# Linear attention and a gated feed-forward layer on one core: two batches' tail rows together, batch 0's k through two DMA queues, and a new order of the first batch

## The chip, the core and the metric

The kernel runs on 1 core of one Trainium2 chip. The metric is the device time of one execution in microseconds (us). TensorE (PE) multiplies matrices, VectorE (DVE) and ScalarE (ACT) work on elements, GpSimd (POOL) issues nearly all loads here, and SyncE (SP) issues the stores and the transposing DMAs. The engines run at the same time, each through its own list of instructions in order, and wait for each other through semaphores.

## The reference

Shapes: 8 batches, 8 heads, 576 rows, head size 64; the feed-forward layer takes 4608 rows of 512, widens them to 2048 and goes back to 512. Inputs and output are float32.

```python
phi = lambda x: np.where(x > 0, x, np.exp(x) - 1.0) + 1.0
q_p, k_p = phi(q), phi(k)
kv  = np.einsum('bhsd,bhse->bhde', k_p, v);  z = np.sum(k_p, axis=2)
num = np.einsum('bhsd,bhde->bhse', q_p, kv)
den = np.einsum('bhsd,bhd->bhs', q_p, z)[..., None] + 1e-06
x = (num / den).transpose(0, 2, 1, 3).reshape(4608, 512)
h = x @ w_in
g = h * (1.0 / (1.0 + np.exp(-beta * h)))
out = g @ w_out
```

## The kernel before

**Tiles.** The 576 rows of a batch are 4 tiles of 128 rows (t = 0..3) and a tail of 64 rows (t = 4). The main rows go through the feed-forward layer batch by batch. The 8 tails are collected in `xT_tail` (512 columns) and go through it at the end as a ninth "batch" (b = 8).

**Stages.** The order is written out by hand (`tc.manual_schedule()`). For each b there is a stage h(b): 16 groups of 128 hidden columns, 4 matmuls each into a PSUM bank, then Silu on ACT into `g_sb` (`h_mm` L453, `silu` L445). Then stage y(b): 64 matmuls with `w_out` (`y_mm` L505), four results of 128x512, copied and stored. A dictionary (`plan`) says after which group a piece of the next batch's attention is put: `relu`, `exp_`, `phi`, `v_copy` (v with a column of ones, `vaug`), `kv_mm` (L344, sums of k and v, with `kv_evac` into `kv_bd`), then for each tile t `num_mm` (L399: four matmuls), `num_norm` (three DVE instructions, L413 to L415, giving `xs`), and the transposition of `xs`: by PE in batches 0 to 2 (`x_trans` L433 and a copy L370 or L372), by a DMA of SP from batch 3 on (L419). The tail of each batch does the same with 64 rows, and ends in 64 columns of `xT_tail`.

**Loads.** All loads but that of beta are issued by POOL, and they cast float32 to bfloat16 on the way; the order is that of the text: k, q and v of batch 0 (in pieces, `load_nine` L129), four `w_in`, `w_out` in eight pieces of float32 (some lie for a while in buffers of later batches: `xqk[2]`, `xT[1]`, `xT[2]`, `g_sb[1]`), k and q of batch 1, v of batch 1, then batch 2 and so on. A load waits until the one eight places before it has landed. `w_out_scale` (L212) turns float32 `w_out` into bfloat16 on DVE.

**The start.** Batch 0 is split into 9 rows per partition (j = 0..8) with 4 heads in each half of the partitions, so that every load is wide. k comes as one piece of 9 rows for each half, q as j 0..3 and j 4..8, v as j 0..5 and j 6..8. ACT makes `exp` (L256), DVE `relu` (L264) and the minimum (L270); PE adds up k (L307 with `ones`), transposes q (L282), adds up k and v (L307 with `v9`); ACT and DVE empty the banks. Meanwhile PE runs matmuls on zeros (`warm`, L575). `beta` is loaded by SP, transposed by PE at the start and worked up by five small DVE instructions (`make_beta`, L199 to L205). On DVE the `relu` of q's second part (L264) comes ahead of the first `num_norm`.

Of the kernel before, what the change touches and what calls it, by code (L numbers as in the profile page):

```python
# [16 lines left out]
def kernel(  # L17
# [99 lines left out]
    def nine(a, spec):  # L117

        names = " ".join(spec)
        flat = a.rearrange("p a b c -> p (a b c)")  # L120
        size = {"h": HH, "j": N9, "d": D}
        n = size["h"] * size["j"] * size["d"]
        return flat[:, 0:n].rearrange(f"p ({names}) -> p {names}", **size)

    q9 = nine(xqk[0][:, 0], "hjd")
    k9 = nine(xqk[0][:, 1], "hjd")
    v9 = nine(vraw[0], "hjd")

    def load_nine(dst, src, h0=0, h1=HH, j0=0, j1=N9):  # L129
        for g in range(2):  # L130
            nc.gpsimd.dma_start(  # L131
                out=dst[g * TAIL : (g + 1) * TAIL, h0:h1, j0:j1, :].rearrange(
                    "p h j d -> p h (j d)"
                ),
                in_=src[0, g * HH + h0 : g * HH + h1, :, :]
                .rearrange("h (p j) d -> p h j d", j=N9)[:, :, j0:j1, :]
                .rearrange("p h j d -> p h (j d)"),
            )
# [3 lines left out]
    nc.scalar.activation(small[:, 0:1], small[:, 0:1], ACTF.Exp)  # L142
    nc.vector.memset(g_sb[0][:, FC - 1, :], 0.0)  # L143
    clear_tail(1)
    nc.vector.memset(vraw[1][TAIL:P, :, NJ, :], 0.0)
    beta_row = consts.tile([FC, P], F32)
    nc.sync.dma_start(out=beta_row, in_=moe_beta.rearrange("(c p) -> c p", p=P))

    identity = consts.tile([P, P], BF16)
    ident16 = consts.tile([FC, FC], F32)  # L150
    load_nine(k9, k)
    load_nine(q9, q, j1=4)
    make_identity(nc, identity)
    make_identity(nc, ident16)
    load_nine(v9, v, j1=6)
    load_nine(v9, v, j0=6)
    load_nine(q9, q, j0=4)
    for i in range(4):
# [88 lines left out]

    x0 = {0: q9, 1: k9}

    def work9(tag, **kw):  # L250
        return nine(work.tile([P, H, NT, D], BF16, tag=tag, name=tag, **kw), "jhd")

    def exp0(a, j0, j1):
        if j0 == 0:
            st["e0", a] = work9("e", bufs=3)
        nc.scalar.activation(  # L256
            st["e0", a][:, j0:j1].rearrange("p j h d -> p h j d"), x0[a][:, :, j0:j1],
            ACTF.Exp,
        )

    def relu0(a, j0, j1):
        if j0 == 0:
            st["r0", a] = work9("r")
        nc.vector.tensor_scalar(  # L264
            st["r0", a][:, j0:j1].rearrange("p j h d -> p h j d"), x0[a][:, :, j0:j1],
            0.0, 1.0, ALU.max, ALU.add,
        )

    def phi0(a, j0, j1):
        nc.vector.tensor_tensor(  # L270
            st["p0"][a][:, j0:j1], st["r0", a][:, j0:j1], st["e0", a][:, j0:j1], ALU.min
        )

    def q_trans0(t, banks, c0):


        for jj in range(2 if t < NJ else 1):
            for a in range(2):
                for g in range(2):
                    gs = slice(g * TAIL, (g + 1) * TAIL)  # L280
                    m0 = c0 + a * P + jj * TAIL
                    nc.tensor.matmul(  # L282
                        banks[:, g, m0 : m0 + TAIL],
                        st["p0"][0][gs, 2 * t + jj, 2 * a : 2 * a + 2, :],
                        identity[gs, gs],
                        is_transpose=True, start=True, stop=True, skip_group_check=True,
                    )

    def q_out0(t, banks, c0, dve):
        n = rows(t)  # L290
        src = banks[:, :, c0 : c0 + 2 * P].rearrange("p g (a n) -> p g a n", a=2)
        dst = st[0, "qT"][:, t].rearrange("p (g a) n -> p g a n", g=2)
        copy(dst[:, :, :, :n], src[:, :, :, :n], dve)

# [4 lines left out]
    def kv_mm0(kvp, j0, j1, of_v):  # L299


        for j in range(j0, j1):
            for a in range(2):
                for g in range(2):
                    gs = slice(g * TAIL, (g + 1) * TAIL)
                    cols = kv_cols(kvp, g, a)
                    nc.tensor.matmul(  # L307
                        cols[:, :, 0:D] if of_v else cols[:, :, D],
                        st["p0"][1][gs, j, 2 * a : 2 * a + 2, :],
                        v9[gs, 2 * a : 2 * a + 2, j, :] if of_v else ones[gs],  # L310
                        start=(j == 0 and a == 0 and not of_v),
                        stop=(j == N9 - 1 and a == 1 and of_v),
                        skip_group_check=True,
                    )

    def kv_evac0(kvp):
        for g in range(2):
# [75 lines left out]
    def num_mm(b, t):  # L393
        n = rows(t)
        nps = att_banks()
        st[b, "n", t] = nps
        for p in range(KC):
            c0 = (p % 2) * 2 * (D + 1)
            nc.tensor.matmul(  # L399
                nps[:n, p // 2, c0 : c0 + 2 * (D + 1)],  # L400
                st[b, "qT"][:, t, p, :n],
                kv_bd[b % 2][p // 2][:, p % 2],
                start=True, stop=True, skip_group_check=True,
            )

    def num_norm(b, t):
        n = rows(t)
        den = work.tile([P, 2, 4], F32, tag="den", name="den")
# [8 lines left out]
        )  # L417
        if by_dma(b):
            nc.sync.dma_start_transpose(  # L419
# [3 lines left out]
    def x_dst(b, t):  # L423
        if t < NJ:
            return xT[b % 3][:, t]
        return xT_tail[:, :, b * TAIL : (b + 1) * TAIL]

    def x_trans(b, t, wide=False, dve=False):
        n = rows(t)
        xv = st[b, "xs", t].rearrange("p a h d -> p (a h d)")  # L430
# [49 lines left out]

    out0 = out[0:S, :].rearrange("(p j) m -> p j m", j=N9)

    def tail_rows(b):
        if b == 0:
            return out0[:, N9 - 1, :]
        return out[b * S + MAIN : (b + 1) * S, :]

    def store(b, t, y_sb):
        if b < B:
            if b == 0:  # L490
                for i in range(2):
                    nc.sync.dma_start(
                        out=out0[:, 2 * t + i, :], in_=y_sb[i * TAIL : (i + 1) * TAIL, :]
                    )
# [88 lines left out]
    def F(f, *a, **k):  # L583
        return lambda: f(*a, **k)

    begin(0)
    st["warm"] = mm_bank([P, 512])
    warm(10)
    beta_trans()
    make_beta()  # L590
    warm(20)
    st["p0"] = [
        nine(st[0, "p"][:, a].rearrange("p j (h d) -> p j h d", h=H), "jhd")
        for a in range(2)
    ]
    exp0(1, 0, 5)
    exp0(1, 5, N9)
    exp0(0, 0, 4)
    relu0(1, 0, 5)
    relu0(1, 5, N9)  # L600
    phi0(1, 0, 5)
    relu0(0, 0, 4)
    phi0(1, 5, N9)
    phi0(0, 0, 4)
    kvp = [mm_bank([P, 512]) for _ in range(2)]
    kv_mm0(kvp, 0, N9, False)
    qb = att_banks(BF16)
    q_trans0(0, qb, 0)
    q_trans0(1, qb, 256)
    q_out0(0, qb, 0, False)  # L610
    q_out0(1, qb, 256, False)
    kv_mm0(kvp, 0, 6, True)
    kv_mm0(kvp, 6, N9, True)
    kv_evac0(kvp)
    st["warm"] = mm_bank([P, 512])
    warm(1)
    num_mm(0, 0)
    num_mm(0, 1)
    exp0(0, 4, N9)
    relu0(0, 4, N9)  # L620
    silu_table()
    num_norm(0, 0)
    phi0(0, 4, 6)
    warm(4)
    x_trans(0, 0, dve=True)
    qb2 = att_banks(BF16)
    q_trans0(2, qb2, 0)
    q_out0(2, qb2, 0, False)
    num_norm(0, 1)
    phi0(0, 6, N9)  # L630

# [4 lines left out]

    def tidy0():
        clear_tail(0)
        nc.vector.memset(vraw[0][TAIL:P, :, NJ, :], 0.0)

    def q_rest0():
        q_trans0(3, qb2, 256)
        q_trans0(4, qb2, 512)
        q_out0(3, qb2, 256, False)
        q_out0(4, qb2, 512, False)

# [5 lines left out]
        {  # L652
            3: [F(x_trans, 0, 1), F(num_mm, 0, 2), F(num_norm, 0, 2), F(q_rest0)],
            5: [F(num_mm, 0, 3), F(num_norm, 0, 3)],
            7: [F(x_trans, 0, 2)],
            8: [F(num_mm, 0, 4), F(num_norm, 0, 4)],
            9: [F(x_trans, 0, 3), F(tidy0)],
            12: [F(x_trans, 0, 4)],
            17: [F(w_out_scale, 0), F(w_out_scale, 1)],
# [33 lines left out]
            1: [F(x_trans, 1, 3)],  # L693
            3: [F(x_trans, 1, 4)],
            8: [F(begin, 2), F(relu, 2, 0)],
# [12 lines left out]
        11: [F(num_mm, 2, 0), F(num_norm, 2, 0)],  # L708
        12: [F(num_mm, 2, 1), F(num_norm, 2, 1), F(x_trans, 2, 0, wide=True)],
        13: [F(num_mm, 2, 2), F(num_norm, 2, 2), F(x_trans, 2, 1, wide=True)],  # L710
        14: [F(num_mm, 2, 3), F(num_norm, 2, 3)],
    })

    for b in range(2, B + 1):
# [3 lines left out]
        if b == 2:  # L718
# [3 lines left out]
            plan = {  # L722
                0: [F(x_trans, 2, 2), F(num_mm, 2, 4), F(num_norm, 2, 4)],
                1: [F(x_trans, 2, 3)],
                3: [F(x_trans, 2, 4)],
            }
# [14 lines left out]
        if n < B:  # L741
            for t in range(NT):
                plan[1 + 2 * t] = [F(num_mm, n, t)]
# [32 lines left out]
```

## Time and profile before

| what | value |
|---|---|
| median of 5 runs (lowest to highest) | 296.69 us (296.07 to 297.36) |
| profiled execution, its own time | 296.69 us |
| span of that execution in the profile | 294.9 us |
| busy time: PE / DVE / ACT / POOL | 283.6 / 124.0 / 175.0 / 52.4 us |
| moved by POOL's queue / by SP's queue | 20.45 / 16.20 MB |

The page of the profile gives busy times of the engines, the span in 40 slices of 7.37 us, and the chain of waits that ended last. A timeline lists the instructions in order of time: start, length, engine, line, what is written and read, and in brackets how long the engine had been idle and which engine or DMA ended that. Matmuls overlap each other in the records, so the length of one is not what it costs in a row of many; the chain shows what a row costs. The span leaves out 1.79 us of the execution's time.

### The profile page before, as it was taken

The numbers are of one execution on the slowest core, as the hardware profiler recorded it, in microseconds if no ns is written. First come the engines' busy times: TensorE is split into PE (matmuls) and PEld (weight loads), VectorE is DVE, ScalarE is ACT, GpSimd is POOL, SyncE is SP. The second block draws the span as 40 slices with busy tenths as digits, with TensorE's granted clock in tenths as the row PEclk, the third lists the DMA queues.
The fourth block names the chain that finished last, engine by engine and source line by source line (L and its number), as shares of the span: only waits on it lengthen the run. The fifth ranks groups of instructions, "written<-read, shape, count | busy, mean of one in ns | idle before, by whom it ended". The sixth has DMA issues, their size and how long they took to land.

```text
span 294.9 us, 4750 instructions
## 1 busy us (share of the span) xinstructions
PE 283.6 (96%) x1891; PEld 143.8 (49%) x1912; DVE 124.0 (42%) x261; ACT 175.0 (59%) x234; POOL 52.4 (18%) x72
## 2 busy tenths in 40 slices
PE   8779999999899999999999999999999999999994
PEld 3457445644465544445444544454445444444444
DVE  4675488504365174616461646164715400110012
ACT  2798786889988770778077808790770077018500
POOL 8824575540003200320033000000000000000000
PEclk9999999999999999999999999999999999999999
DMA  7999999999637993699369955024502400120032
GB/s 103 189 207 345 253 278 192 257 192 191 94 142 101 175 137 107 129 179 150 98 129 159 161 107 124 2 72 115 127 0 72 118 36 0 38 90 16 0 73 71
DMA packets 72310, 37.09 MB, mean 126 GB/s; under 512 B 40912, under 2 KB 66784, under 8 KB 72288
## 3 DMA queue, kind: packets, MB, share of 16 engines
q0 software_dynamic: 38912, 20.45, 47.8%
q1 hardware_dynamic: 33216, 16.20, 23.1%
q8 instruction: 15, 0.25, 0.3%
q10 hardware_dynamic: 160, 0.13, 0.2%
q14 instruction: 7, 0.06, 0.1%
HBM read 36.71 MB, written 9.44 MB: 156 GB/s over the span
## 4 chain that ended last, share of the span: by engine, by line
PE 76%; ACT 9%; DMA 7%; issue 3%; POOL 2%; DVE 2%; ACTq 0%; POOLq 0%
PE mm L453 36%; PE mm L505 33%; DMA vraw<-in_v_dram 5%; ACT e L229 3%; PE att L399 3%; DMA xqk<-in_q_dram 2%; PE att L344 1%; ACT g L445 1%; ACT L229 1%; PE mm L537 1%; PE att L453 1%; POOL xqk L131 1%; ACT L581 1%; POOL vraw L131 1%; DVE qk_p L242 0%
## 5 line engine op out<-in xcount | busy, mean ns | idle before, releaser
L445 ACT ACTIVATE g<-mm,beta_c 128x512 bf16<-128x512 f32 (+2 forms) x156 | 97.3, 633 | 87.9 <-PE mm L453 87.7
L505 PE MATMUL mm<-w_out,g 128*128 128x512 bf16 x541 | 126.7, 379 | 1.2 <-issue 0.3
L453 PE MATMUL mm<-xT,w_in 128*128 128x512 bf16 (+2 forms) x560 | 108.1, 349 | 0.6 <-DVE xT L370 0.3
L453 PEld LDWEIGHTS <-w_in 128*128 128x128 bf16 x656 | 61.9, 98 | 61.5 <-DMA w_in<-in_moe_w_in_dram 0.4
L505 PEld LDWEIGHTS <-g 128*128 128x128 bf16 x560 | 52.8, 97 | 58.3
L515 DVE COPY y_sb<-mm 128x512 f32<-128x512 f32 x27 | 18.7, 692 | 70.5 <-PE mm L505 69.1
L229 ACT ACTIVATE e<-xqk 128x2560 bf16<-128x2560 bf16 x14 | 31.9, 2329 | 0.1
L415 DVE TENSOR_TENSOR xs<-att,rden 128x512 bf16<-128x512 f32 (+1 forms) x40 | 27.6, 690 | 1.4
L242 DVE TENSOR_TENSOR qk_p<-r,e 128x2560 bf16<-128x2560 bf16 x14 | 20.9, 1490 | 13.1 <-ACT e L229 12.4
L72 POOL DMA_DIRECT2D vraw<-in_v_dram x7 | 7.0, 998 | 84.2 <-DVE vaug L370 78.4
L355 DVE CAST kv_bd<-att 64x130 bf16<-64x130 f32 x28 | 8.2, 292 | 32.2 <-PE att L344 31.8
L413 DVE TENSOR_SCALAR den<-att 128x8 f32<-128x8 f32 (+1 forms) x40 | 6.5, 162 | 31.4 <-PE att L399 31.2
L399 PE MATMUL att<-kv_bd,q_pT 128*128 128x130 bf16 (+1 forms) x160 | 15.8, 221 | 1.5 <-DVE kv_bd L370 0.7
L399 PEld LDWEIGHTS <-q_pT 128*128 128x128 bf16 (+1 forms) x160 | 11.6, 100 | 11.1 <-DVE xs L415 2.4
L453 PE MATMUL mm<-xT_tail,w_in 128*128 128x512 bf16 x63 | 13.9, 379 | 0.1
L237 DVE TENSOR_SCALAR r<-xqk 128x2560 bf16<-128x2560 bf16 x14 | 11.6, 836 | 3.7 <-DMA xqk<-in_q_dram 2.2
L575 PE MATMUL mm<-g 128*128 128x512 bf16 x34 | 9.4, 435 | 1.2 <-DVE g L143 1.2
L229 ACT ACT_TABLE_LOAD x7 | 9.0, 1283 | 0.1
L414 DVE RECIPROCAL rden<-den 128x8 f32<-128x8 f32 (+1 forms) x40 | 8.1, 201 | 1.4
L256 ACT ACTIVATE e<-xqk 128x1280 bf16<-128x1280 bf16 (+1 forms) x4 | 4.4, 1155 | 5.9 <-DMA xqk<-in_k_dram 5.3
L72 POOL DMA_DIRECT2D xqk<-in_k_dram x7 | 6.8, 977 | 5.5 <-DMA w_in<-in_moe_w_in_dram 2.0
L72 POOL DMA_DIRECT2D xqk<-in_q_dram x7 | 6.3, 900 | 6.3 <-ACT g L445 2.6
(71 smaller groups left out, 140.2 us busy)
## 6 DMA issues: line engine op xcount, KB each, us to landing
out_dram<-y_sb SPq DMA_DIRECT2D x28, 256.0 KB, 2.3
xqk<-in_k_dram POOLq DMA_DIRECT2D x7, 512.0 KB, 10.7
xqk<-in_q_dram POOLq DMA_DIRECT2D x7, 512.0 KB, 11.6
vraw<-in_v_dram POOLq DMA_DIRECT2D x7, 512.0 KB, 11.3
w_in<-in_moe_w_in_dram POOLq DMA_DIRECT2D x4, 512.0 KB, 10.8
g<-in_moe_w_out_dram POOLq DMA_DIRECT2D x4, 512.0 KB, 10.9
out_dram<-y_sb SPq DMA_DIRECT2D x14, 128.0 KB, 5.2
xqk<-in_moe_w_out_dram POOLq DMA_DIRECT2D x2, 512.0 KB, 14.4
```

Source lines behind the costliest of these rows:

```text
L72: eng.dma_start(out=dst[:, :, 0:NJ, :].rearrange("p h j d -> p h (j d)"), in_=src[b, :, 0:MAIN, :].rearrange("h (p j) d -> p h (j d)", j=NJ),)
L229: nc.scalar.activation(st[b, "e", a][:, h0:h1], xqk[b % NX][:, a, h0:h1], ACTF.Exp)
L237: nc.vector.tensor_scalar(st[b, "r", a][:, h0:h1], xqk[b % NX][:, a, h0:h1], 0.0, 1.0, ALU.max, ALU.add)
L242: nc.vector.tensor_tensor(st[b, "p"][:, a].rearrange("p j (h d) -> p h j d", h=H)[:, h0:h1], st[b, "r", a][:, h0:h1], st[b, "e", a][:, h0: ...
L355: nc.vector.tensor_copy(kv_bd[b % 2][i][gs, :, g, :], st[b, "kvp"][gs, 2 * i : 2 * i + 2, :])
L399: nc.tensor.matmul(nps[:n, p // 2, c0 : c0 + 2 * (D + 1)], st[b, "qT"][:, t, p, :n], kv_bd[b % 2][p // 2][:, p % 2], start=True, stop=True ...
L415: nc.vector.tensor_mul(xs[:n], nv[:, :, :, 0:D], rden[:n, :, :, None].to_broadcast([n, 2, 4, D]))
L445: nc.scalar.activation(g_sb[b % 2][:, ff, c0:c1], hp[:, c0:c1], ACTF.Silu, scale=beta_c[:, ff : ff + 1],)
L453: nc.tensor.matmul(hp[:, c0:c1], w_in_sb[ff // 4][:, kc, (ff % 4) * P : (ff % 4 + 1) * P], x[:, t0:t1, kc, :] if b < B else x[:, kc, c0:c1 ...
L505: nc.tensor.matmul(yp, g_sb[b % 2][:, ff, t * P : (t + 1) * P], w_out_sb[ff // 4][:, ff % 4, :], start=(ff == 0), stop=(ff == FC - 1),)
L515: nc.vector.tensor_copy(y_sb, yp)
L575: nc.tensor.matmul(st["warm"], g_sb[0][:, FC - 1, 0:P], g_sb[0][:, FC - 1, :], start=True, stop=True, skip_group_check=True,)
```

## The change

- **Joint tails.** The tails of batches 2i and 2i+1 are worked on together: `num_mm` of the tail is called for the odd batch alone, and issues eight matmuls, alternately for batch 2i (rows 0 to 63 of the bank) and 2i+1 (rows 64 to 127). One `num_norm` with 128 rows follows, and one transposing DMA of SP into 128 columns of `xT_tail`, for batches 0 to 2 too, whose tails PE transposed before.
- **k by two queues.** k of batch 0 is cut into j 0..4, loaded by POOL as before, and j 5..8, loaded by SP without a cast as float32 into a part of `g_sb[1]` (`k_last`). `beta` is loaded by ACT's queue instead of SP's. v is cut at 5 instead of 6.
- **Order in batch 0.** `make_beta` comes behind the minimum; 25 instead of 30 matmuls on zeros; the minimum of q's first part in two pieces; the sums over k's first part ahead of those over its second; q's tile 1 is transposed behind the sums. The first `num_norm` comes ahead of the `relu` of q's second part. In h(0) the pieces lie after other groups, and q's tiles 2 to 4 are transposed together, two of them copied by DVE.
- **Batch 2.** All four copies behind `x_trans` go to DVE; the second `x_trans` comes one place later.
- In POOL's list every load stands where it stood.

```diff
+    k_last = g_f[:, 0 : HH * (N9 - KF) * D].rearrange(
+        "p (h j d) -> p h j d", h=HH, j=N9 - KF
+    )
...
+    load_nine(k_last, k, KF, N9, eng=nc.sync)
...
-    nc.sync.dma_start(out=beta_row, in_=moe_beta.rearrange("(c p) -> c p", p=P))
+    nc.scalar.dma_start(out=beta_row, in_=moe_beta.rearrange("(c p) -> c p", p=P))
...
-    load_nine(k9, k)
-    load_nine(q9, q, j1=4)
+    load_nine(x9[1][:, :, 0:KF], k, 0, KF)
+    load_nine(x9[0][:, :, 0:QF], q, 0, QF)
...
     def num_mm(b, t):
-        n = rows(t)
         nps = att_banks()
         st[b, "n", t] = nps
         for p in range(KC):
             c0 = (p % 2) * 2 * (D + 1)
-            nc.tensor.matmul(
-                nps[:n, p // 2, c0 : c0 + 2 * (D + 1)],
-                st[b, "qT"][:, t, p, :n],
-                kv_bd[b % 2][p // 2][:, p % 2],
-                start=True, stop=True, skip_group_check=True,
-            )
+            for i in range(1 if t < NJ else 2):
+                bb, n, r0 = (b, P, 0) if t < NJ else (b - 1 + i, TAIL, i * TAIL)
+                nc.tensor.matmul(
+                    nps[r0 : r0 + n, p // 2, c0 : c0 + 2 * (D + 1)],
+                    st[bb, "qT"][:, t, p, :n],
+                    kv_bd[bb % 2][p // 2][:, p % 2],
+                    start=True, stop=True, skip_group_check=True,
+                )
...
-        if by_dma(b):
+        if by_dma(b) or t == NJ:
...
-        return xT_tail[:, :, b * TAIL : (b + 1) * TAIL]
+        return xT_tail[:, :, (b - 1) * TAIL : (b + 1) * TAIL]
...
+    num_norm(0, 0)
-    exp0(0, 4, N9)
-    relu0(0, 4, N9)
+    exp9(0, QF, N9)
+    relu9(0, QF, N9)
     silu_table()
-    num_norm(0, 0)
-    phi0(0, 4, 6)
     warm(4)
     x_trans(0, 0, dve=True)
+    num_norm(0, 1)
+    phi9(0, QF, 6)
+    phi9(0, 6, N9)
     qb2 = att_banks(BF16)
-    q_trans0(2, qb2, 0)
-    q_out0(2, qb2, 0, False)
-    num_norm(0, 1)
-    phi0(0, 6, N9)
...
-            3: [F(x_trans, 0, 1), F(num_mm, 0, 2), F(num_norm, 0, 2), F(q_rest0)],
-            5: [F(num_mm, 0, 3), F(num_norm, 0, 3)],
-            7: [F(x_trans, 0, 2)],
-            8: [F(num_mm, 0, 4), F(num_norm, 0, 4)],
-            9: [F(x_trans, 0, 3), F(tidy0)],
-            12: [F(x_trans, 0, 4)],
+            1: [F(x_trans, 0, 1)],
+            3: [F(q_rest)],
+            5: [F(num_mm, 0, 2), F(num_norm, 0, 2)],
+            7: [F(num_mm, 0, 3), F(num_norm, 0, 3)],
+            8: [F(x_trans, 0, 2)],
+            10: [F(x_trans, 0, 3, dve=True), F(tidy)],
...
             1: [F(x_trans, 1, 3)],
-            3: [F(x_trans, 1, 4)],
...
-        12: [F(num_mm, 2, 1), F(num_norm, 2, 1), F(x_trans, 2, 0, wide=True)],
-        13: [F(num_mm, 2, 2), F(num_norm, 2, 2), F(x_trans, 2, 1, wide=True)],
-        14: [F(num_mm, 2, 3), F(num_norm, 2, 3)],
+        12: [F(num_mm, 2, 1), F(num_norm, 2, 1), F(x_trans, 2, 0, wide=True, dve=True)],
+        13: [F(num_mm, 2, 2), F(num_norm, 2, 2)],
+        14: [
+            F(x_trans, 2, 1, wide=True, dve=True), F(num_mm, 2, 3), F(num_norm, 2, 3),
+        ],
...
-                0: [F(x_trans, 2, 2), F(num_mm, 2, 4), F(num_norm, 2, 4)],
-                1: [F(x_trans, 2, 3)],
-                3: [F(x_trans, 2, 4)],
+                0: [F(x_trans, 2, 2, dve=True)],
+                1: [F(x_trans, 2, 3, dve=True)],
...
-            for t in range(NT):
+            for t in range(NT if n % 2 else NJ):
```

## The prediction

> **What bounds the kernel now.** First the page: the slices, then the chain that ended last by engine.
>
> ```profile
> PE   8779999999899999999999999999999999999994
> PEclk9999999999999999999999999999999999999999
> DMA  7999999999637993699369955024502400120032
> ...
> PE 76%; ACT 9%; DMA 7%; issue 3%; POOL 2%; DVE 2%; ACTq 0%; POOLq 0%
> ```
>
> From about 85 us on PE is the bound (no idle slice but the last, granted clock 1.0 throughout): there only PE work that goes away counts. Before that the DMA engines are busy in every slice to 74 us (ten slices), so I look at that stretch by windows (busy us of each engine, granted clock, share of the 16 DMA engines, GB/s; over 1 because transfers overlap):
>
> ```profile
> 2.00:3.00 1.00, 1.00 (x4) 0.39 (x3) 0.89 (x4) 0.23 (x2) 1.00 (x3) 1.00 0.34 25
> 3.00:5.00 2.00, 2.00 (x7) 0.61 (x5) 0.71 (x7) 0.00 (x0) 1.85 (x7) 1.00 1.03 141
> 5.00:7.50 2.50, 2.50 (x13) 1.21 (x13) 0.95 (x5) 0.00 (x0) 2.50 (x5) 1.00 1.23 187
> 17.00:42.00 25.00, 24.52 (x188) 14.88 (x190) 15.10 (x30) 22.02 (x39) 11.87 (x15) 1.00 1.29 276
> 42.00:52.00 10.00, 9.18 (x110) 5.55 (x110) 8.67 (x22) 6.00 (x10) 6.68 (x8) 1.00 1.50 211
> 52.00:74.00 22.00, 21.95 (x152) 11.82 (x153) 6.74 (x9) 19.65 (x29) 6.71 (x7) 1.00 1.53 213
> ```
>
> One queue feeds them without a hole from 3 us on; before 3 us they are nearly empty. Then the timeline, at the places where PE waits for a load:
>
> ```profile
> 7.52 1.27 ACT L256 ACTIVATE e<-xqk 128x1280 bf16<-128x1280 bf16 x1 [5.28 <-DMA xqk<-in_k_dram]
> ...
> 16.92 0.90 PEld L453 LDWEIGHTS <-w_in 128*128 128x128 bf16 x16 [0.41 <-DMA w_in<-in_moe_w_in_dram]
> ...
> 42.18 0.83 DVE L370 COPY vaug<-vraw 128x2560 bf16<-128x2560 bf16 x1 [0.42 <-DMA vraw<-in_v_dram]
> ...
> 43.06 0.82 PE L344 MATMUL att<-vaug,qk_p 128*64 128x65 bf16 x40 [0.20 <-DVE vaug L370]
> ...
> 79.49 0.40 PE L399 MATMUL att<-kv_bd,q_pT 128*128 128x130 bf16 x4 [0.66 <-DMA q_pT<-qk_p]
> ```
>
> k is in at 7.5; h(0) starts at 16.9 when `w_in` and the first `xT` arrive together; in y(0) PE needs batch 1's v (landed 42.05) for `kv_mm` at 43.06; in y(1) it needs batch 2's transposed q at 79.49. So the kernel is three stretches: to 43 us loads, then PE with one wait for a transposing DMA, then PE alone. The sum is made against the profiled execution, 296.69 us for a span of 294.9; the median of the five runs is the same 296.69.
>
> **The change part by part.**
>
> *k by two queues.* Beta, alone on SP's queue, is issued at 0.75 and the trace's packet records show it moving at 2.05; k's first packets on POOL's queue move at 2.96. So a second queue can start 0.9 us earlier, in the empty window. Against it stands more packet work. The records give, per packet, 0.107 us for 1152 bytes (0.145 in the first half of k), 0.072 for 640 bytes, 0.060 for 512 bytes (which read 1024 bytes), 0.098 for 1024 bytes (which read 2048). k was 512 x 0.107 = 54.8 engine-us. It becomes 512 x 0.072 plus 512 float32 packets of 1024 bytes, which no load of before has: between 0.060 and 0.098, so 67.6 to 87.0. The sum rises by 12.8 to 32.2 engine-us, at about 20 per us (share 1.23 x 16) 0.6 to 1.6 us. The cut of v gives 0.1 back, and the slow first half of k (256 x 0.038 / 19 = 0.5 us) may fall into the empty window. Best: 0.9 + 0.5 + 0.1 - 0.6 = 0.9 us gained; worst: 0.9 + 0.1 - 1.6 = 0.6 lost. I take 0.6 gained: the 512-byte packet reads as many bytes, so it is the nearest row. As the DMA engines have no hole until 74 us and POOL's list is unchanged, every later load moves by this, batch 1's v too: **-0.6 us**.
> The Trainium skill (DMA: Bandwidth & Descriptors, "Issuing engines are not separate DMA queues") speaks against this: a second issuing engine saves only issue time, since all share 16 DMA engines. By the rule the term would be near nothing, which is the first rival; the row that bears on it is the empty window from 2 to 3 us.
>
> *First norm ahead, new order in h(0).* On DVE the `relu` of q's second part (0.61 us, waiting for its load to 14.18) goes from in front of `den` to behind `xs`; the xT copy would end near 15.5 instead of 16.87. Next late is `w_in` at 16.87 - 0.6: h(0) starts near 16.3. Inside h(0) the tail's four `num_mm` (0.35 in the chain) and its `x_trans` (0.22) go, eight transpositions of q's tile 2 come in (0.29). The waits for `xT` and `q_pT` (0.26, 0.16) may go or come. PE would reach y(0) a us or more early, but PE already waited at 43.06 for v of batch 1, and that comes 0.6 early only. So beyond the loads this is worth **0**; without the cover (v early) it would be 0.5 to 1. The same cover hides a late start of up to half a us.
> At nothing too: beta's issue on ACT (idle to 7.52; were beta later than PE's 5.08, only matmuls on zeros wait); `make_beta`, 1.08 us, on DVE while it idled 1.52 us before the `kv_bd` copy at 12.93; `relu` from float32, by the `w_out` scaling (0.44 for 512 columns) 0.9 instead of 0.56 for 1024, beside ACT's three `exp` of 3.2 us; five fewer zero matmuls. New waits: PE now stands before v's first part with k's second sums and q's transposition queued behind, done before v's second part lands at about 12. A later `kv_bd` delays `xT`, which has 0.8 us until `w_in`.
> PE idles somewhat more between 9 and 16 us; the trace shows clock 1.00 there with PE busy for 3.1 of 5 us (12 to 17). The Trainium skill (TensorE: Matmul & The Clock Gate, "Part 1: The HAM clock gate") says that about 3.4 us of idleness halves the clock. No gap that I work out is so long; by the rule nothing is lost.
>
> *Joint tails.* What four of them cost, from the chain, in order of time:
>
> ```profile
> 97.74 0.75 PE att L344 x40
> ...
> 110.74 0.35 PE att L399 x4
> ```
>
> A pair of tails cost 0.70. Eight alternating matmuls of 130 columns: at most 0.70 again; at least as L344, which alternates between the same halves: 0.75/(40 x 65) = 0.29 ns a column, so 0.30. I take 0.40, near L344, with the 0.12 that four tail matmuls cost over four full ones (0.23) added. In h(1): 0.35 and an `x_trans` of 0.22 become 0.40: **-0.2** (-0.27 to +0.13). Batches 3 to 7, all on PE's path: 5 x 0.35 = 1.75 becomes 3 x 0.40 = 1.20: **-0.55** (-0.85 to +0.35). The norms and DMAs saved lie beside PE work.
>
> *Batch 2.* h(2) loses its tail `num_mm` and `x_trans`; PE took 2.97 us from 85.08 to 88.05, of which 16 matmuls (1.74) and two `x_trans` (0.44) stay: up to 0.8 less. In y(1) ACT is busy with `exp` and table until 81.7, and PE waited 0.29 for ACT's xT copy at 82.91; with the copies on DVE the chain is three norms (1.13 each) and copies (0.42), and h(2) starts 0.1 earlier: together **-0.85** (-0.57 to -0.9).
>
> *The wait at 79.49.* q's transposing DMA was issued at 70.14 and landed 9.3 us later (5.6 in the median), beside POOL's loads, which run to 74.8. After: the issue comes 0.8 earlier, the loads' end only 0.1, because the new transposing DMA of tails 0 and 1 (512 packets of 0.023 us, 0.5 us of all engines) goes among them. 0.7 us more overlap; I count half: **+0.35** (-0.3, if the wait goes, to +0.7).
>
> "Loads of batch 2 not held back": each stands in POOL's list where it stood, and waited for loads ahead of it (1.9 us at 36.4), so nothing beyond the term above.
>
> Sum: -0.6 - 0.2 + 0.35 - 0.85 - 0.55 = -1.85; 296.69 - 1.85 = **294.8 us**.
>
> **The rivals.**
> 1. *The second queue wins nothing*, as the DMA engines are shared. For: the saturated windows. Against: the empty one. Without the 0.6 the sum is -1.25: 295.4; at its bad end 296.0.
> 2. *The eight matmuls don't overlap.* A pair costs 0.70: h(1) +0.13, later batches +0.35. Sum -0.6 + 0.13 + 0.35 - 0.85 + 0.35 = -0.6: 296.1. Against: L344.
> 3. *Slower: two queues get in each other's way.* If all packets of k take 0.145 us, as its first half did, k costs 148 engine-us instead of 65, 83/19 = 4.4 us more, less 0.9 of early start: batch 1's v lands 3.5 us late, and PE stands at `kv_mm`. +3.5 - 0.2 - 0.85 - 0.55 = +1.9: 298.6. It decides from v 1.6 us late (no gain); beyond 2.5 it is slower by 0.9 us. For: two rings at a time have not been seen in this stretch. Against: from 5 us on, three loads queued together move at full rate.
>
> **How the numbers follow.** This kernel's measurement tells 0.3% (0.9 us) from no change: below 295.8 is faster, above 297.6 slower. Forecast 0.62, rival 1 0.15, rival 2 0.10, rivals 1 and 2 together 0.03, rival 3 0.10. Faster: 0.59 of the forecast, 0.09 of rival 1, 0.03 of rival 2: 0.71. Slower: 0.10. Same: 0.19. All good ends together give -0.9 - 0.27 - 0.3 - 0.9 - 0.85 = -3.2: 293.5 at the low end; all bad ends +1.2: 297.9. I stop at 297.2, leaving out rival 3 and the last of the bad ends.
>
> **What would show it.** First `exp` before 7.0 instead of 7.52; `w_in` awaited no longer than 16.4; PE's `kv_mm` of batch 1 near 42.4, waiting for v; `num_mm` of batch 2 near 79.0; h(2) from 84.4, its second half from about 86.7; the entries for tails in the chain become one for two batches, of about 0.40; the period of two batches from 101 us shorter by 0.3. I am wrong if batch 1's v does not land earlier, or if PE's waits between 43 and 85 us grow.

## The result and the profile after

| | before | changed kernel |
|---|---|---|
| median of the runs (lowest to highest) | 296.39 us (296.05 to 297.36, 45 runs) | 297.92 us (295.87 to 299.0, 25 runs) |
| ratio to before, 95% interval | | 1.004 (1.0029 to 1.0051) |
| profiled execution / its span | 296.69 / 294.9 us | 298.14 / 296.4 us |

The change makes the kernel slower by 0.4%, 1.5 us; 294.8 was predicted, and the highest time of the range was 297.2. The first part of the page that answers to the one shown of before (busy tenths and granted clock in 40 slices of 7.41 us, then the chain by engine):

```profile
PE   8889999999599999999999999999999999999994
...
PEclk9899999999989999999999999999999999999999
DMA  8999999999924996599359955023502400020032
...
PE 88%; DMA 6%; DVE 2%; POOL 2%; issue 1%; POOLq 0%
```

PE has a slice of 5 where it had 9: the eleventh, 74 to 81.5 us. The slice behind it shows a lower clock, and so does the second. The DMA engines are full in the eleventh slice too (9, was 6). The windows (columns as before: busy us of PE, PEld, DVE, ACT, POOL, then clock, DMA share, GB/s) put sizes to it:

```profile
2.00:3.00 1.00, 1.00 (x4) 0.39 (x3) 0.89 (x4) 0.23 (x2) 1.00 (x2) 1.00 0.55 101
...
12.00:17.00 5.00, 4.17 (x39) 2.32 (x39) 2.94 (x11) 4.12 (x7) 2.77 (x4) 0.66 1.25 206
...
42.00:52.00 10.00, 9.64 (x114) 5.98 (x114) 8.56 (x22) 5.96 (x11) 6.09 (x8) 1.00 1.53 200
...
78.00:82.00 4.00, 0.42 (x5) 0.43 (x6) 0.00 (x0) 2.84 (x3) 0.00 (x0) 0.86 0.55 67
81.00:85.00 4.00, 3.42 (x19) 2.07 (x20) 1.62 (x6) 0.60 (x1) 0.00 (x0) 0.59 0.00 0
```

The second queue does fill the window from 2 to 3 us (DMA share 0.55, was 0.34). From 42 to 52 PE works more than before (9.64, was 9.18). From 78 to 82 PE stands, with half of the DMA engines busy, and from 81 to 85 it runs at a clock of 0.59. The same places in the timeline as before:

```profile
7.68 1.27 ACT L269 ACTIVATE e<-xqk 128x1280 bf16<-128x1280 bf16 x1 [5.45 <-DMA xqk<-in_k_dram]
...
17.14 0.62 PE L477 MATMUL mm<-xT,w_in 128*128 128x128 bf16 x8 [0.72 <-DMA w_in<-in_moe_w_in_dram]
...
41.37 0.83 DVE L391 COPY vaug<-vraw 128x2560 bf16<-128x2560 bf16 x1 [0.39 <-DMA vraw<-in_v_dram]
...
42.52 0.82 PE L365 MATMUL att<-vaug,qk_p 128*64 128x65 bf16 x40
...
53.96 1.39 SPq L443 DMA_TRANSPOSE xT_tail<-xs  x1
...
69.10 7.00 SPq L409 DMA_TRANSPOSE q_pT<-qk_p  x1
...
81.58 0.62 PE L423 MATMUL att<-kv_bd,q_pT 128*128 128x130 bf16 x4 [3.76 <-DMA q_pT<-qk_p]
```

To 69 us the changed kernel is ahead: batch 1's v lands 0.8 us earlier (41.37, was 42.18), and q's transposing DMA is issued 1.0 earlier (69.10, was 70.14). But PE waits for that DMA to 81.58, 3.76 us instead of 0.66: it takes 12.4 us to land, not 9.3. The chain of waits (start, length, what) shows what this is worth:

```profile
69.10 12.43 DMA q_pT<-qk_p
...
82.19 1.71 PE mm L529 x4
...
88.46 0.44 PE mm L477 x4
...
100.17 0.75 PE att L365 x40
...
113.17 0.35 PE att L423 x8
```

Four `y_mm` at 82.19 take 1.71 us; in a row at full clock four take 0.86. h(2) starts at 88.46, 3.2 later than before, where the chain has it at 85.25:

```profile
85.25 0.44 PE mm L453 x4
```

Then the gains come: `kv_mm` of batch 3 is 2.4 late (100.17 against 97.74), and the end 1.5 late. The eight tail matmuls cost 0.35, what four did. So all of the loss arises between 69 and 88 us, at q's DMA and right behind it.

### The profile page after: what moved, and what is told of

It reads as the page before. It is cut to its first block, busy times and chain, and to the rows that moved or that the text cites. A ratio compares the mean times of both kernels' runs of the same rounds, so it can differ in the third digit from the quotient of the medians.

```text
span 296.4 us, 4705 instructions
## 1 busy us (share of the span) xinstructions
PE 283.5 (96%) x1874; PEld 143.4 (48%) x1895; DVE 122.3 (41%) x257; ACT 171.5 (58%) x225; POOL 51.5 (17%) x72
## 4 chain that ended last, share of the span: by engine, by line
PE 88%; DMA 6%; DVE 2%; POOL 2%; issue 1%; POOLq 0%
PE mm L477 40%; PE mm L529 37%; DMA q_pT<-qk_p 4%; PE att L423 4%; PE att L477 2%; DMA vraw<-in_v_dram 2%; PE att L365 2%; PE mm L561 1%; DVE xs L439 1%; POOL xqk L135 1%; PE mm L457 1%; PE mm L599 1%; POOL vraw L135 1%; PE att L401 0%; DVE rden L438 0%
## 5 line engine op out<-in xcount | busy, mean ns | idle before, releaser
L245 DVE TENSOR_TENSOR qk_p<-r,e 128x2560 bf16<-128x2560 bf16 x14 | 20.9, 1491 | 12.4 <-ACT e L232 11.7
L439 DVE TENSOR_TENSOR xs<-att,rden 128x512 bf16<-128x512 f32 x36 | 24.9, 691 | 1.5 <-DVE rden L438 0.2
L437 DVE TENSOR_SCALAR den<-att 128x8 f32<-128x8 f32 x36 | 5.9, 163 | 32.7 <-PE att L423 32.5
L423 PE MATMUL att<-kv_bd,q_pT 128*128 128x130 bf16 (+1 forms) x160 | 15.2, 230 | 4.0 <-DMA q_pT<-qk_p 3.8
L537 ACT ACTIVATE y_sb<-mm 128x512 f32<-128x512 f32 x8 | 4.8, 597 | 7.6 <-PE mm L529 7.6
L438 DVE RECIPROCAL rden<-den 128x8 f32<-128x8 f32 x36 | 7.3, 203 | 1.2
```

The lines of the kernel that those rows point to most:

```text
L245: nc.vector.tensor_tensor(st[b, "p"][:, a].rearrange("p j (h d) -> p h j d", h=H)[:, h0:h1], st[b, "r", a][:, h0:h1], st[b, "e", a][:, h0: ...
L423: nc.tensor.matmul(nps[r0 : r0 + n, p // 2, c0 : c0 + 2 * (D + 1)], st[bb, "qT"][:, t, p, :n], kv_bd[bb % 2][p // 2][:, p % 2], start=True ...
L439: nc.vector.tensor_mul(xs[:n], nv[:, :, :, 0:D], rden[:n, :, :, None].to_broadcast([n, 2, 4, D]))
```

## The experiments

The kernel before ran beside each group at 296.35 to 296.63 us. Theory A was: the transposing DMA of tails 0 and 1 (L443, issued at 53.96), which runs among the loads, delays them so far that their end meets q's transposing DMA. The expectations name its rivals.

**1. Tails 0 and 1 transposed by PE again.**

```diff
-        if by_dma(b) or t == NJ:
+        if by_dma(b) or (t == NJ and b > 1):
...
             1: [F(x_trans, 1, 3)],
+            3: [F(x_trans, 1, 4)],
```

> The changed kernel, but the joint tail of batches 0 and 1 is transposed by PE in h(1) again (four matmuls, one copy of ACT), not by a DMA of SP. Theory A (that DMA, issued at 54 us among the saturated loads, makes the loads end about 3 us later; they then overlap q's transposing DMA of batch 2, PE stands 3.8 us at its num_mm and the clock halves): PE's wait there under 1.2 us, loads' end near 75 us, clock 1.0 after 80 us, time 294.0 to 294.9. Theory B (not the tail's DMA but the earlier start of everything, by k's second queue, makes stores, loads and q's transposing DMA meet): the wait stays near 3.8 us, time 297 to 298. Theory C (the half clock from 12.9 to 16.3 us in the first batch costs the time): 297 to 298.

Measured: 294.32 us (294.21 to 294.45), ratio 0.9924 (0.991 to 0.9939). This one DMA costs 3.6 us (297.92 - 294.32). In this profile q's DMA is awaited for no time at all (in those of experiments 2, 6 and 8, which have no DMA of tails among the loads either, for 0.78 to 0.94 us):

```profile
78.86 0.41 PE L423 MATMUL att<-kv_bd,q_pT 128*128 128x130 bf16 x4
```

**2. The same DMA, but issued behind q's.**

```diff
+    def tail_dma(b):
+        xs = st[b, "xs", NJ]
+        nc.sync.dma_start_transpose(
+            out=x_dst(b, NJ), in_=xs.rearrange("p a h d -> p (a h d)")
+        )
...
-        1: [F(phi, 2, 0), F(q_trans_dma, 2), F(phi, 2, 1)],
+        1: [F(phi, 2, 0), F(q_trans_dma, 2), F(tail_dma, 1), F(phi, 2, 1)],
```

> The changed kernel, but the transposing DMA of the tails of batches 0 and 1 is issued by SP behind q's transposing DMA of batch 2 instead of ahead of it, when the loads are over. Theory A: as if PE had done it, and 0.2 us less PE work: wait under 1.2 us, 293.8 to 294.7. Theory B and C: 297 to 298.

Measured: 294.41 us, ratio 0.9926 (0.9911 to 0.9941). The DMA costs nothing where the loads have ended: its place is the price, not its work. In this profile the clock was halved from 10.85 to 14.26 us, and nothing was lost; so the lower clock in slice 2 of the changed kernel need not cost anything.

**3. Joint tails alone, on the kernel before.** The diff's edits to `num_mm`, `num_norm` and `x_dst` and the tail entries of the plans; nothing of the start, nor of batch 2's copies.

> The kernel before with joint tails alone (all four pairs, transposed by DMAs of SP; one queue for k, old order of batch 0, ACT's copies in batch 2). Theory A: the wait of PE at num_mm of batch 2 grows from 0.7 to 3 us or more, time 296.8 to 298.0 though PE has less to do. Theory B: the wait stays near 0.7 us, and the PE work saved (tails of batches 2, 4, 6 and one transposition, together 1.2 to 1.6 us) shows: 294.8 to 295.4.

Measured: 298.06 us (296.59 to 299.62), ratio 1.0042 (1.002 to 1.0064). The whole loss is there without any other part of the change, with the same wait in the timeline:

```profile
81.67 0.40 PE L402 MATMUL att<-kv_bd,q_pT 128*128 128x130 bf16 x4 [3.70 <-DMA q_pT<-qk_p]
```

**4. PE kept warm in the gaps at 10 to 16 us.**

```diff
+    warm(3)
```

(ahead of each of the two parts of the sums over k and v of batch 0)

> The changed kernel with three more matmuls on zeros ahead of each part of the sums over k and v, where PE waits for v. Theory C: the granted clock stays 1.0 from 5 to 17 us and the time falls by 1 us or more, below 297. Theory A and B: the clock may stay up at 13 us, but h(0) waits for w_in and y(0) for batch 1's v anyway; the wait at num_mm of batch 2 stays near 3.8 us, time 297.3 to 298.3.

Measured: 297.87 us, ratio 1.003 (1.0006 to 1.0054). The clock is 1.00 from 12 to 17 us and the time does not move. With the second experiment, the clock at the start is out.

The next four start from the first experiment's kernel (294.32 us) and test the other terms of the sum.

**5. k by one queue.**

```diff
-    load_nine(k_last, k, KF, N9, eng=nc.sync)
...
-    load_nine(x9[1][:, :, 0:KF], k, 0, KF)
+    load_nine(x9[1], k, 0, N9)
```

> The changed kernel with the first pair's tails transposed by PE (as in the run that did this alone, 294.3 us), and k of batch 0 loaded in one piece of nine rows by POOL as before; the minimum, the sums and v's cut stay new. The prediction's term for the second queue: 0.6 us lost, 294.9. Rival (the second queue wins nothing in the end): 294.1 to 294.5, h(0) at most 0.3 us later.

Measured: 294.79 us (294.62 to 295.27), ratio 0.9935. The second queue is worth 0.47 us. h(0) starts at 17.26, and `kv_mm` of batch 1, which waits for the copy of v as the prediction had it, at 43.27. In the ten profiles with the second queue both come earlier, but a single profile says little about how much: 15.89 to 17.14 (15.89 in the first experiment's) and 42.33 to 43.06 (43.06).

**6. `relu` of q's second part ahead of the first norm again.**

```diff
-    num_norm(0, 0)
     exp9(0, QF, N9)
     relu9(0, QF, N9)
+    num_norm(0, 0)
```

> As the run with the first pair's tails transposed by PE (294.3 us), with the first num_norm behind the relu of q's second part on DVE again. The prediction's step (hidden, because w_in and then batch 1's v are late anyway): no change, 294.1 to 294.5. Rival (it moves the start): 0.5 us or more lost, 294.8 or above.

Measured: 294.37 us (293.93 to 294.64), ratio 0.992. The order is worth nothing.

**7. A plain DMA in the place of the transposing one.** `xs` of tails 0 and 1, 128 KB, into a tile that nobody reads; PE transposes as well.

```diff
+        if b == 1 and t == NJ:
+            nc.sync.dma_start(out=scratch, in_=xs.rearrange("p a h d -> p (a h d)"))
```

> As the run with the first pair's tails transposed by PE (294.3 us), and at the place of their transposing DMA a plain DMA of SP copies the same 128 KB into an unused tile. Theory A1 (it is the transposing kind of DMA that stops the loads: DMA idle for 0.6 us at 59.4 us and its 512 packets spread over 3.2 us): little loss, 294.2 to 294.9, PE's wait for q under 1.3 us. Theory A2 (any further 128 KB on SP's queue among the loads does it): loads' end near 77 us or later, wait above 2 us, 296 or above.

Measured: 295.02 us (294.72 to 297.08, 12 runs), ratio 0.9954 (0.9938 to 0.997). The same bytes at the same place cost 0.7 us instead of 3.6. They move here as 128 packets of 1024 bytes, 7.9 engine-us by the packet records, where the transposing DMA has 512 packets of 256 bytes, 15.8 engine-us when nothing stops them (experiments 11 and 12). So how much of the difference is due to the transposing, and how much to the smaller packets, is not separated. The profiled execution was the slowest of these, 297.08, with a wait of 2.47 us, and behind it the clock fell (0.84 in this window, at half for 3.41 us from 80.69):

```profile
80.32 0.40 PE L423 MATMUL att<-kv_bd,q_pT 128*128 128x130 bf16 x4 [2.47 <-DMA q_pT<-qk_p]
...
80.00:81.00 1.00, 0.68 (x6) 0.49 (x7) 0.20 (x2) 0.89 (x2) 0.00 (x0) 0.84 0.00 0
```

So a plain DMA too can end in the wait; why it did in that execution stays open.

**8. Batch 2's copies by ACT, at the old places.**

```diff
-        12: [F(num_mm, 2, 1), F(num_norm, 2, 1), F(x_trans, 2, 0, wide=True, dve=True)],
-        13: [F(num_mm, 2, 2), F(num_norm, 2, 2)],
+        12: [F(num_mm, 2, 1), F(num_norm, 2, 1), F(x_trans, 2, 0, wide=True)],
+        13: [F(num_mm, 2, 2), F(num_norm, 2, 2), F(x_trans, 2, 1, wide=True)],
...
-                0: [F(x_trans, 2, 2, dve=True)],
-                1: [F(x_trans, 2, 3, dve=True)],
+                0: [F(x_trans, 2, 2)],
+                1: [F(x_trans, 2, 3)],
```

> As the run with the first pair's tails transposed by PE (294.3 us), with batch 2's four xT copies on ACT again and its second x_trans at its old place. The prediction's step (PE waited 0.3 us for ACT's copy, h(2) starts 0.1 us later): 294.3 to 294.6. Rival (ACT's copies hold up the start of h(2)): 0.5 us or more lost.

Measured: 294.66 us (294.49 to 295.15), ratio 0.9934. The copies on DVE are worth 0.3 us.

**9. Matmuls in the wait.** On the changed kernel.

```diff
         st[b, "n", t] = nps
+        if b == 2 and t == 0:
+            for _ in range(13):
+                nc.tensor.matmul(
+                    nps[:, 0, :], g_sb[1][:, 0, 0:P], g_sb[1][:, 0, :],
+                    start=True, stop=True, skip_group_check=True,
+                )
```

> The changed kernel with 13 more matmuls of 512 columns, on data that nobody reads afterwards, directly ahead of batch 2's first num_mm in y(1), so that PE works on in most of the 3.8 us (77.8 to 81.6) in which it stood for q's transposing DMA. 13 x 0.22 = 2.9 us, so nothing that has to be done is held up while the DMA lands after 80.7. Theory (the idleness halves the clock behind it, and that is a cost of its own): the wait ends near 81.6 as before, no row at half clock at 81 us, h(2) starts at about 87.0 instead of 88.3, and the time falls by about 1.3 us, to 296.6. Rival (the clock behind the wait costs nothing that matters, because the next wait takes it up): time 297.9, the start of h(2) stays at 88.3.

Measured: 296.9 us (296.45 to 297.56), ratio 1.0008 (0.9994 to 1.0021): 1.0 us less than the changed kernel. The window that had a clock of 0.59 has 1.00, and PE does 29 instructions in it instead of 19:

```profile
81.00:85.00 4.00, 3.82 (x29) 2.07 (x29) 3.01 (x10) 1.78 (x4) 0.00 (x0) 1.00 0.17 66
```

By the chain h(2) starts at 86.79 here, 1.7 earlier, although the real `num_mm` come at 81.19, only 0.4 earlier. So about 1.0 us of the median, 1.3 in the two profiles (1.7 - 0.4), is the halved clock behind the wait.

The mean granted clock of the runs agrees; one stretch of 3.41 us at half clock lowers it by 0.006. In the fourth experiment, whose start is kept warm, the four runs at 1.000 took 296.22 to 296.61 us and the six at 0.989 to 0.994 took 297.84 to 299.13. Of the changed kernel's runs the six at 0.999 or 1.000 took 296.16 to 297.20, and the nine at 0.988 or 0.989, with two such stretches, 297.60 to 299.00 (the ten between, with one stretch wherever it lay, 295.87 to 298.47). Between the medians lie 1.9 and 1.6 us; a longer wait is part of that, beside the clock.

**10. Joint tails alone, tails 0 and 1 by PE.** The third experiment's kernel with the first one's edit.

> The kernel before with the joint tails alone, but with the pair of batches 0 and 1 transposed by PE and copied, as the tails were before: no transposing DMA among the loads. Against the joint tails with the transposing DMA (298.06) this takes away only that DMA. Theory (that DMA's price among the loads is the whole of the loss; joint tails gain 0.8 in h(2) and 0.55 to 0.93 in batches 3 to 7): no wait above 0.9 at batch 2's num_mm, loads end within half a us of the kernel before, time 296.5 - 1.35 to 1.75 = 294.8 to 295.2. Rival (joint tails themselves win little, and the gain seen with the whole change comes from the new order and the second queue): 296.0 to 296.6.

Measured: 295.38 us (294.96 to 295.7), ratio 0.9955 (0.994 to 0.9971). Without that DMA the joint tails gain 1.2 us, with it they lose 1.4: again about 2.7 us for one DMA. 0.2 us above the expectation.

**11 and 12. The same DMA a little later.** Why so much? The windows of 0.5 us around its packets, first of the changed kernel, then of the kernel with the plain DMA, show a hole:

```profile
59.00:59.50 0.50, 0.50 (x4) 0.19 (x2) 0.00 (x0) 0.50 (x1) 0.00 (x0) 1.00 3.15 93
59.50:60.00 0.50, 0.50 (x4) 0.23 (x3) 0.00 (x0) 0.32 (x2) 0.00 (x0) 1.00 0.14 15
```

```profile
59.00:59.50 0.50, 0.50 (x4) 0.21 (x3) 0.00 (x0) 0.50 (x1) 0.33 (x1) 1.00 1.42 192
59.50:60.00 0.50, 0.50 (x5) 0.20 (x3) 0.00 (x0) 0.32 (x2) 0.50 (x1) 1.00 1.43 195
```

15 GB/s where loads move at 195, and a share of 3.15 just before: that counts packets that began there and did not end. The records of single packets say which:

```
packets of the changed kernel      start     length
queue "instruction", 16384 bytes   58.22     0.97
xT_tail<-xs, 512 x 256 bytes       58.22 to 61.43, usually 0.031
  17 of them                       59.06 to 59.43, up to 0.96
```

One packet of the instruction queue moves 16384 bytes in about 1 us. In the kernels with the hole (the changed one, 3, 4 and 9) it falls into the transposing DMA, and towards its end 17 or 18 of the small packets begin to stand, the longest of each kernel for 0.9 to 1.3 us. With the plain DMA the same packet (58.36, 0.93 us) meets no stop. Theory D: the packets of a transposing DMA go in step over the 16 engines; where one engine is held, the other 15 stand until it has caught up, and the loads queued on them stand too. (The records do not say on which engine a packet ran.) Two kernels move the DMA behind that packet by working on the joint tail five and seven half groups later in h(1):

```diff
-            0: [F(x_trans, 1, 2), F(num_mm, 1, 4), F(num_norm, 1, 4)],
+            0: [F(x_trans, 1, 2)],
             1: [F(x_trans, 1, 3)],
+            5: [F(num_mm, 1, 4), F(num_norm, 1, 4)],
```

> The changed kernel with the joint tail of batches 0 and 1 (eight num_mm, norm, transposing DMA) five half groups later in h(1), 0.44 us each: the DMA is issued near 55.9 instead of 53.96 and its 512 packets should move near 60.5 to 63.5 instead of 58.46 to 61.67, in the same saturated loads, but behind the one packet of 16384 bytes of the instruction queue (58.46, 0.97 us in the changed kernel; 59.00, 0.93 in the joint tails alone). New theory D: the emptiness at 59.5 to 60.3 comes of these two meeting: one DMA engine is held by the 16384-byte packet, the transposing DMA's packets go in step over the 16 engines, and the other 15 stand until the one has caught up. Then no packet of the transposing DMA takes over 0.3 us here, the loads' bytes lose only what the 512 packets take themselves (512 x 0.031 = 16 engine-us, 1 us), the wait at batch 2's num_mm is below 2, and the time is 294.9 to 295.7. Rival (any transposing DMA among saturated loads empties the engines): packets of 0.8 us and more and an empty stretch inside its own 3 us again, loads to 78.5 or later, the wait 3 to 3.8, time 297.5 to 298.2.

> The same seven half groups later: issue near 56.9, packets near 61.4 to 64.5, farther from the 16384-byte packet at 58.5 to 60 and ahead of the next instruction packet (8192 bytes at 66.3). Theory D: as with five half groups, no long packets, wait below 2, 294.9 to 295.7. Rival (any transposing DMA there): wait 3 to 3.8, 297.5 to 298.2. A third outcome: no emptiness, but loads that still end after 78 and a wait above 2.5; then the emptiness is not what delays the loads, but the mixing of the packets itself.

Measured: 295.9 us (295.28 to 297.92), ratio 0.9992 (0.9974 to 1.0011), and 295.55 us (295.13 to 298.12), ratio 0.9976 (0.996 to 0.9992). The first is 0.2 above D's range, the second within it. The packets now move at 61.02 to 63.26 and 62.33 to 64.99, the longest takes 0.03 us, the windows of 1 us around them show 175 to 197 GB/s and no hole, and PE's wait in the timeline is half of what it was, in the first

```profile
79.97 0.40 PE L423 MATMUL att<-kv_bd,q_pT 128*128 128x130 bf16 x4 [1.78 <-DMA q_pT<-qk_p]
```

and in the second kernel:

```profile
80.49 0.40 PE L423 MATMUL att<-kv_bd,q_pT 128*128 128x130 bf16 x4 [1.83 <-DMA q_pT<-qk_p]
```

In the second, an instruction packet of 8192 bytes (64.10, 0.58 us) lay within the DMA and stopped nothing; whether it was too short, or D is not the whole account, is open.

How far the loads were behind is seen in the KB that POOL's queue had still to move at 70 us (from the packet records; at full rate it moves some 190 KB a us; the profiles of 1, 2, 6 and 8, with the same loads and no DMA of tails among them, lie between 620 and 640):

| kernel | KB left at 70 us | against its twin without the DMA | wait at batch 2's `num_mm` |
|---|---|---|---|
| 1 (tails by PE) | 639 | | 0 |
| 7 (plain DMA) | 716 | +77 | 2.47 |
| 11, 12 (DMA moved) | 776, 881 | +137, +242 | 1.78, 1.83 |
| changed kernel | 953 | +313 | 3.76 |
| 10 (joint tails alone, by PE) | 685 | | 0.90 |
| 3 (joint tails alone) | 1007 | +322 | 3.70 |

So the DMA's price has three parts. It takes the loads' turns, hole or not: 137 to 242 KB, 0.7 to 1.3 us. The meeting with the instruction packet adds some 70 to 185 KB, up to 1 us. And what is late at 70 us grows while the last loads and q's own transposing DMA share the engines (q's packets move from 73.17 to 80.92 us in the changed kernel, from 72.62 to 76.84 in the first experiment's), and behind a long wait the clock halves: after 2.47 us in the seventh experiment's profile, after 3.70 and 3.76 in those of the third and of the changed kernel, not after 1.78 and 1.83 in those of 11 and 12.

D is supported by the two moves and by the plain DMA. Other places bear it out in part: in all 14 traces, behind 20 us, an instruction packet of 16384 bytes lies 29 times beside 100 or more packets of a transposing DMA. In 27 of these 4 to 19 of the small packets take over 0.4 us; in two, one of them at 77.46 us in experiment 11, none or one does. Only in eight are they 14 or more, so that all the engines stand is not shown as the rule.

The changed kernel's runs spread over 3 us (295.87 to 299.0), those without the DMA over a quarter of a us (294.21 to 294.45). About half of that goes with the clock behind the wait (experiment 9). Why the wait is long in one run and shorter in the next was not shown; that transfers meet more or less closely from run to run would do it.

## Why the prediction was wrong

**The step that failed** is "The wait at 79.49", which took the new transposing DMA as "512 packets of 0.023 us, 0.5 us of all engines" and made +0.35 of it, with +0.7 as the worst. The direction and the mechanism (the loads' end against q's DMA) were right; the size was not. Measured: 3.6 us by the first experiment, 2.7 by the third and the tenth. Three things were missing. The packets' own time is not what they cost the loads: in a mixed stretch a packet took 0.031, and the loads lost 0.7 us and more where 0.5 was reckoned. The halt behind an instruction packet was put at nothing. At that place before had no transposing DMA, but its trace has such a halt elsewhere: at 92.07 to 92.36 us, in q's DMA of batch 3, 19 packets take up to 1.66 us behind an instruction packet of 91.73, and from 92.5 to 93 the engines move 1 GB/s. And the loss was counted half ("I count half"), while at q's DMA it grows: the loads' last packet ended at 78.69 instead of 75.68 (the prediction's 74.8 is the landing of v's large piece; the small one landed at 75.98), q's DMA landed at 81.53 instead of 79.45, and then the clock fell.

**The clock.** "No gap that I work out is so long; by the rule nothing is lost" meant the gaps of the first batch. None there is longer than 0.64 us (from 5.8 us until the clock fell), and yet the clock was halved from 12.64 to 16.05 us, with PE busy for 2.2 of the 3.4 us before. Nothing was lost (experiments 2 and 4), but not by the rule. The halving that did cost, behind q's DMA, followed from the mis-sized wait: PE stood for 3.76 us, the records show half clock for 3.41 us from 80.90, and it made about 1.0 us of the loss (experiment 9). The Trainium skill (TensorE: Matmul & The Clock Gate, "Part 1: The HAM clock gate") gives an idle window of some 3.4 us; the wait of 3.76 agrees with it, but the wait of 2.47 us in experiment 7 and the gaps of the first batch were shorter, and the clock fell all the same.

**The other terms held.** Without the failed term the sum was -2.2; the first experiment gives 296.39 - 294.32 = 2.1, or 2.3 against its own runs of before (296.63). h(2) starts there at 84.47 by the chain, where the prediction's sign said "from 84.4".

- *k by two queues*, -0.6: -0.47 measured. But the steps under it were off both ways: SP's k moves from 2.28, half a us later than beta did before (1.79), and POOL's from 3.17 instead of 2.72 (counted from the span's start as the other views are; the prediction's 2.05 and 2.96 are about 0.25 too high), so the first `exp` came at 7.68 and not before 7.0 (7.16 to 7.68 in the ten profiles with the second queue). On the other side the packets were cheap, by the medians 0.049 for 1024 bytes and 0.069 for 640 (512 x 0.118 = 60 engine-us, 5.6 more than the prediction's 54.8; 12.8 at least were reckoned). The prediction mixed two measures here: 54.8 is 512 times the median packet, while all records of k before sum to 64.9, the 65 of its rival 3; in the changed kernel they sum to 72.3. Rival 1 falls, by half a us. Rival 3 falls: v of batch 1 came 0.8 earlier, and in none of the ten profiles later than before.
- *First norm ahead*, 0: 0.05 (experiment 6), within the noise.
- *Joint tails.* The pair costs 0.35, below the 0.40 taken; rival 2 falls. Between `kv_mm` of batch 3 and the end the changed kernel makes up 2.43 - 1.5 = 0.9 us, where 0.55 was predicted, near the best end (0.85).
- *Batch 2*, -0.85: from h(2)'s start to `kv_mm` of batch 3 the changed kernel takes 0.8 less (3.2 - 2.4). The copies, put at 0.1, were 0.3 by themselves.

The prediction's test was apt: "I am wrong if [...] PE's waits between 43 and 85 us grow." One grew, by 3.1 us. No rival had it: all three looked at the start or at the matmuls. The slower one should have been this: the new DMA delays the loads by more than its own packets, and decides from some 2 us of added wait on, where the 2.1 us of gains are eaten.

## What to carry to other kernels

A small DMA put among saturated loads costs what it does to the chain behind them, not its own packets' time: follow the loads' end to the next transfer that must wait for it, and take the worst case whole, not half. Put transposing DMAs where the load queue is empty, or let PE transpose: both gave 294.3 to 294.4 us here, 0.8% better than before, with all other parts of the change kept. And where PE's wait may grow to 2.5 us, add the halved clock behind it.

## What the runs showed of the hardware

- A transposing DMA can stop where an instruction packet of 16384 bytes (0.93 to 0.97 us) lies in it: in the four traces with the hole 17 or 18 of its packets take up to 0.9 to 1.3 us instead of 0.031. Some groups of long packets, such as 73.58 to 74.28 in the kernel before, have no instruction packet beside them; what holds these is open.
- The Trainium skill (Advanced Engine Details and Errata, "X-Bar Transpose (TRN2)") says that transpose DMAs are as fast as regular ones. Beside loads the same 128 KB cost 0.7 us as a plain DMA of 1024-byte packets and 3.6 us as a transposing one of 256-byte packets, 1.2 to 1.6 where no instruction packet met it. Behind the loads it cost nothing.
- PE's clock was halved behind a single wait of 2.47 us, and in the first batch with no gap over 0.64 us.
- Eight matmuls of 64 columns of weights, alternating between the two halves, cost 0.35 us, as much as four.
